# Gate rows moved from GpSimd to VectorE, dwo tiles and loads in another order: one change to a fused attention and MLP gradient kernel

## The chip, the cores and the metric

The kernel runs on one core of a Trainium2 chip. A core has five engines, each with its own instruction queue: TensorE (PE, matmuls; PEld are its weight loads), VectorE (DVE), ScalarE (ACT), GpSimd (POOL) and SyncE (SP, which here only issues DMAs). Matmul results land in PSUM, a small accumulation memory; everything else is in SBUF or in device memory. An engine runs its own queue in order and waits for others by semaphores. The metric is the time of one execution in device microseconds; a run gives the median of several executions.

## What is computed

The reference is the forward pass and all gradients of a block that multiplies an attention branch with a gated MLP branch (2048 rows, 512 channels, 32 heads of 16, hidden size 1792):

```python
def _A_ref(x, wqkv, wo):                       # attention
    q, k, v = split_heads(x @ wqkv)
    p = softmax(einsum("bhqd,bhkd->bhqk", q, k) * Dh ** -0.5)
    return merge_heads(einsum("bhqk,bhkd->bhqd", p, v)) @ wo
def _B_ref(x, w1, b1, w2, b2):                 # MLP
    h = gelu(layernorm(x) @ w1 + b1)
    return h @ w2 + b2
xn  = layernorm(x)
out = x + _A_ref(xn, wqkv, wo) * silu(_B_ref(xn, w1, b1, w2, b2))
# results: out, and the gradients of x, wqkv, wo, w1, b1, w2, b2 for a given grad_out
```

## The kernel before

Rows are handled in 16 tiles of 128 ("row t"), in four groups of four. The program has three parts, each written in a fixed order by hand; nothing is rescheduled.

**First part (`Pre`).** It projects q, k and v and transposes them, computes the MLP's hidden layer (`hid`) and then runs a loop over the 16 rows. For row t, `gate(t)` does 14 matmuls into `ps_m`, adds the bias on DVE (L373), takes tanh on ACT (L374) and runs a chain of three DVE instructions (L375 to L377): `sg`, the gate `G_`, and `dsr`, which is grad_out times the gate (dSO). `gate_b` then makes the gradient factor `B_` with four instructions on POOL (L381 to L384). Two rows later `dproj` multiplies the transposed dSO (`dsoT`) with wo to get dO: four matmuls into `ps_do`, a DVE cast into `ndc` (L393) and a POOL copy into `ND` (L394). `t_do` and `t_ds` transpose dO and dSO on PE, with a copy on ACT (L177). `gate_store` writes `gbr` (GB_s) and `dsr` (DSO_s) to device memory for every second row; `after` writes a group's dO (NATQd_s, DOT_s) and then loads the first head pair's share back (`op0["do"]`, L95 and L98). All these DMAs go through SP's queue, except the last `gate_store`, which goes through POOL's. The gate_b of rows 14 and 15 is kept in a list and issued at the end. An ACT instruction on one element (L446) loads the table for the exponential ahead of attention; it stands behind row 15's tanh.

The tiles `gbr`, `dOT` and `gd` (whose halves are `gw`, with `m_` and `sg`, and `dsr`) have memory that attention's `ek` tiles take over: the first write of such a tile waits for the last reader and the last store of the old one.

**Attention (`attention_core`).** 1024 steps: scores (L1083), exponential on ACT (L1092), dP (L1105) and its product on DVE (L1122), PE transposes (L1167) with their copies into `ek` (L1179), and accumulating matmuls. SP issues DMA transposes of `gts` and `ets`. POOL clears the second operand set first (L47 to L50) and then loads the next head pair, paced by the steps.

**Tail (`Grads.run`).** Rows 2 to 15: `emit_so(t)` multiplies the attention output with wo (`ps_so`), DVE makes `dm_all` (L573) and `t13` (L575), POOL adds x and stores the output for two rows (L584, L586; a ring of two tiles). `emit_oT` and `emit_dmT` are PE transposes with ACT copies. `load_s1` loads the rows' factors. Between rows, four tiles of the gradient of wo (`emit_dwo`, 16 matmuls each, needs all of `dso_all`) are emitted after rows 9, 11, 13 and 14. Then follow 14 tiles of dw2 (`emit_dw2`, each needs an `hgr` tile that SP loads with a DMA transpose, L698), dwq and dwkv (12 tiles, the latter need `dKVn`, eight DMA transposes, L781), and the groups dh (need `w2T`, 14 DMA transposes, L778), dy (need `w1T`, L853), dw1 and dx. Alongside, `slope_step` issues one piece of the derivative of gelu: 49 pieces over 16 chunks of h1 (`load_h1`), with Square and Sigmoid on ACT (L654, L668, L669) and multiplications on DVE (L658 to L675).

All loads of the tail are on SP's queue in the order of the program text, so a load that waits (for its memory to come free, or for an earlier DMA) holds up all behind it.

Of the kernel before, what the change touches and what calls it, by code (L numbers as in the profile page):

```python
# [11 lines left out]
ALU = mybir.AluOpType  # L12
# [89 lines left out]
class Pre:  # L102


    def __init__(self, ctx, tc, k, op0, A_x, A_wqkv, A_wo, B_w1, B_b1, B_w2, B_b2, grad_out):
# [257 lines left out]
        def gate(t):  # L363
            g, t4 = t // 4, t % 4
            ps = psA.tile([128, 512], f32, name="ps_m", tag="mm")
            for fc in range(FC):
                nc.tensor.matmul(ps[:], lhsT=hgT[:, g % 2, fc, t4 * 128:(t4 + 1) * 128], rhs=w2_sb[:, fc, :],  # L367
                                 start=(fc == 0), stop=(fc == FC - 1))
# [5 lines left out]
            nc.scalar.activation(out=ta, in_=m_, func=ACT.Tanh, scale=0.5)  # L374
            nc.vector.tensor_scalar(out=sg, in0=ta, scalar1=0.5, scalar2=0.5, op0=ALU.mult, op1=ALU.add)  # L375
            nc.vector.tensor_tensor(out=G_, in0=m_, in1=sg, op=ALU.mult)
            nc.vector.tensor_tensor(out=dsr[:, t % 4, :], in0=dot, in1=G_, op=ALU.mult)  # L377
            return lambda: gate_b(B_, G_, sg, dot)

        def gate_b(B_, G_, sg, dot):  # L380
            nc.gpsimd.tensor_scalar(out=B_, in0=sg, scalar1=-1.0, scalar2=1.0, op0=ALU.mult, op1=ALU.add)  # L381
            nc.gpsimd.tensor_tensor(out=B_, in0=B_, in1=G_, op=ALU.mult)
            nc.gpsimd.tensor_tensor(out=B_, in0=B_, in1=sg, op=ALU.add)
            nc.gpsimd.tensor_tensor(out=B_, in0=B_, in1=dot, op=ALU.mult)  # L384

        def t_ds(t):
            tp(lambda b: dsr[:, t % 4, b * 128:(b + 1) * 128], dsoT[:, t % 2], 0)
# [8 lines left out]
        def t_do(t):  # L396
            g = (t // 4) % 2
            tp(lambda b: ndc[:, t % 2, b * 128:(b + 1) * 128], dOT[:, g, :, (t % 4) * 128:(t % 4) * 128 + 128], 0)

        def after(t):  # L400
            if t % 4 == 3:
                g = t // 4
                ld(out=k.NATQd_s[:, :, g * 4:g * 4 + 4, :].rearrange("a p t c -> p a t c"), in_=ND[:, g % 2])
                ld(out=k.DOT_s.rearrange("(c p) s -> p c s", p=128)[:, :, g * 512:(g + 1) * 512], in_=dOT[:, g % 2])
                op0["do"](g)

        def gate_store(t, ld=ld):
            if t % 2 == 1:
                ld(out=k.GB_s.rearrange("(t p) x d -> p t x d", p=128)[:, t - 1:t + 1], in_=gbr[:, (t - 1) % 4:(t - 1) % 4 + 2])
                ld(out=k.DSO_s.rearrange("(t p) d -> p t d", p=128)[:, t - 1:t + 1], in_=dsr[:, (t - 1) % 4:(t - 1) % 4 + 2, :])  # L410

        def load_dot(g):
            ld(out=dotr[:, g % 2], in_=go2[:, g * 4:g * 4 + 4])
# [11 lines left out]
        for t in range(NT):  # L425
            g, t4 = t // 4, t % 4
            n0, n1 = (0, 4, 8, 11, 14)[t4:t4 + 2]
            if g < 3:
                for fc in range(n0, n1):
                    hid(g + 1, fc)  # L430
            if t == 4:
                op0["q"]()
            if t >= 1:
                gate_store(t - 1)
            if t == 0:
                bound()
            gb = gate(t)
            if t == 0:
                stores_nat(3)
            if t < 14:  # L440
                gb()
            else:
                lastb.append(gb)
            if t == 15:

                nc.scalar.activation(out=b2bc[0:1, 0:1], in_=b2bc[0:1, 0:1], func=ACT.Exp)  # L446
            if t >= 2:
                dproj(t - 2)
            if t >= 3:
                t_do(t - 3)  # L450
                after(t - 3)
            if t >= 1:
                t_ds(t - 1)
            if t4 == 3 and g + 2 < 4:
                load_dot(g + 2)
            if 2 <= t < 6:
                wkv_rows(t - 2)
        dproj(NT - 2)
        t_do(NT - 3)
        after(NT - 3)  # L460
        t_ds(NT - 1)
        t_do(NT - 2)
        after(NT - 2)
        dproj(NT - 1)
        t_do(NT - 1)
        after(NT - 1)
        for gb in lastb:
            gb()
        gate_store(NT - 1, nc.gpsimd.dma_start)


GA = 0.044715
# [4 lines left out]
class Grads:  # L477
# [119 lines left out]
    def run(self):  # L597
# [99 lines left out]
        def load_hg(fc):  # L697
            tr(out=hgr[:, fc % 4], in_=k.HGT_s[fc * 128:fc * 128 + 128, :])  # L698
# [37 lines left out]
        self.load_s1(2)  # L736
        self.load_s1(3)
        self.load_s1(4)
        load_h1(0, 0)
        load_h1(0, 1)  # L740
        nc.vector.memset(ones_bf[:], 1.0)

        nd = 0
        for t in range(2, NT):
            self.emit_so(t)
            if t + 2 < NT:
                self.emit_oT(t + 2)
            while nd < t and nd <= 2 * (t - 3) + 1:
                emit_dmT(nd)
                nd += 1  # L750
            if t == 3:
                self.load_s1(5)
                ld(out=dso_all[:, 0:8], in_=dsov[:, 0:8])
            if t == 5:
                self.load_s1(6)
                ld(out=dso_all[:, 8:16], in_=dsov[:, 8:16])
                load_h1(0, 2)
            if t == 7:
                self.load_s1(7)
                load_hg(0)  # L760
            if t in (9, 11, 13, 14):
                i = (9, 11, 13, 14).index(t)
                emit_dwo(i)
                (load_hg(i + 1) if i < 3 else load_h1(1, 1))
                (load_h1(0, 3) if i == 0 else load_h1(1, 0) if i == 2 else None)
        self.flush_adds()
        while nd < NT:
            emit_dmT(nd)
# [62 lines left out]
        for i in range(12):  # L831
# [635 lines left out]
```

## Time and profile before

| | us |
|---|---|
| median of three runs | 2234.59 (2231.56 to 2238.38) |
| profiled execution, whole | 2229.55 |
| its span, first to last instruction | 2227.8 |
| mean granted TensorE clock | 0.993 of full speed |

The profile records one execution. A row of a timeline has the start in us from the span's start, the length in us, the engine, the line, the operation, what it writes and reads with its shapes, and the count if neighbours are merged; in brackets stands the idle time of the engine ahead of it and what ended it. "SPq" rows are DMA issues on SP's queue. A row of the windows gives a stretch, its length, the busy time of PE, PEld, DVE, ACT and POOL with instruction counts, the granted PE clock, the DMA engines' busy share and GB/s. The chain of waits follows the work that ended last back from the end.

### The profile page before, as it was taken

The page shows a single profiled execution, that of the slowest core. Times are in us where ns is not written, and L with a number is a line of the kernel's source. Part 1 is how long each engine was busy: PE and PEld are TensorE (multiplying, and loading weights), DVE is VectorE, ACT ScalarE, POOL GpSimd, SP SyncE. Part 2 cuts the span into 40 slices and gives each one's busy share as a digit, 9 for nine tenths or more (in the row PEclk, how much of TensorE's full clock was granted, in tenths as well). Part 3 has the DMA queues.
Part 4 walks back from the last instruction along what each step waited for, and adds up shares of the span by engine and source line. Part 5 has one row for each costly group of instructions (what it writes and reads, how often), then busy time and mean ns, then how long its engine had stood idle before and what let it go on. Part 6 is the DMA issues. An engine that isn't in the chain of part 4 may idle for free.

```text
span 2227.8 us, 74213 instructions
## 1 busy us (share of the span) xinstructions
PE 2158.9 (97%) x30690; PEld 1204.8 (54%) x30690; DVE 1912.6 (86%) x3626; ACT 1734.3 (78%) x2481; POOL 607.5 (27%) x1387
## 2 busy tenths in 40 slices
PE   6999899999999999999999999999999999899998
PEld 3444455555555555555555555555555555344444
DVE  6676799999999999999999999999999998698624
ACT  5664888888888888888888888888888886584214
POOL 4276413222222222222312222222213223310002
PEclk9999999999999999999999999999999999999999
DMA  7785999999999999999999999999999999899874
GB/s 230 245 275 197 190 200 192 199 203 194 202 201 196 201 192 210 196 204 196 202 201 198 200 194 204 197 195 204 199 201 200 196 213 230 233 251 252 231 202 155
DMA packets 1421747, 461.15 MB, mean 207 GB/s; under 512 B 1334622, under 2 KB 1405662, under 8 KB 1421408
## 3 DMA queue, kind: packets, MB, share of 16 engines
q1 hardware_dynamic: 1406880, 424.67, 100.3%
q0 software_dynamic: 12944, 30.16, 5.2%
q8 instruction: 240, 3.93, 0.8%
q10 hardware_dynamic: 1584, 1.57, 0.2%
q14 instruction: 99, 0.81, 0.1%
HBM read 62.79 MB, written 64.75 MB: 57 GB/s over the span
## 4 chain that ended last, share of the span: by engine, by line
PE 89%; DVE 3%; DMA 3%; ACT 3%; issue 2%; SPq 1%; POOL 1%; DVEq 0%; ACTq 0%; POOLq 0%
PE tT L1167 24%; PE d L1105 14%; PE X L1197 10%; PE Z L1281 10%; PE X L1200 5%; PE X L1204 5%; PE s L1083 2%; PE ps_dw L729 2%; PE ps_dy L902 2%; PE ps_m L367 2%; PE ps_h L352 2%; PE ps_dw L974 2%; PE ps_dh L868 2%; PE XT L1223 1%; PE ps_qkv L210 1%
## 5 line engine op out<-in xcount | busy, mean ns | idle before, releaser
L1122 DVE TENSOR_TENSOR gts<-d,ets 128x512 bf16<-128x512 f32 x2048 | 1363.0, 684 | 99.5 <-ACT ek L1179 20.3
L1092 ACT ACTIVATE ets<-s 128x1024 bf16<-128x1024 f32 x1024 | 1048.7, 1024 | 196.9 <-PE s L1083 94.6
L1167 PE MATMUL tT<-ident_bf,ets 128*128 128x128 bf16 x7168 | 569.2, 219 | 15.9 <-ACT ek L1179 6.1
L1167 PEld LDWEIGHTS <-ets 128*128 128x128 bf16 x7168 | 445.7, 97 | 241.2 <-issue 239.3
L1179 ACT COPY ek<-tT 128x448 f32<-128x448 f32 (+2 forms) x1024 | 501.6, 490 | 7.3 <-DVE ek L1179 6.1
L1105 PE MATMUL d<-QDT,KVT 32*128 32x512 bf16 x2048 | 457.4, 385 | 0.0
L1083 PE MATMUL s<-QDT,KVT 32*128 32x512 bf16 x2048 | 401.3, 380 | 3.0 <-ACT ets L1092 2.7
L1105 PEld LDWEIGHTS <-KVT 32*128 32x128 bf16 x2048 | 145.2, 91 | 323.7 <-issue 323.7
L1197 PE MATMUL X<-ets,NAT 128*32 128x256 bf16 x4096 | 300.5, 284 | 0.1
L1204 PE MATMUL X<-gts,NAT 128*17 128x256 bf16 x4096 | 289.8, 273 | 0.0
L1200 PE MATMUL X<-ets,Lc 128*32 128x256 bf16 x4096 | 289.8, 273 | 0.0
L1341 POOL COPY tick<-gts 1x2 bf16<-1x2 bf16 x205 | 36.1, 176 | 604.5 <-DVE gts L1122 604.5
L1281 PE MATMUL Z<-gk,W 128*32 128x512 bf16 x2048 | 197.8, 379 | 1.0 <-DVE acc L1295 1.0
L1281 PE MATMUL Z<-ek,W 128*32 128x512 bf16 x1792 | 198.6, 379 | 0.0
L1246 POOL TENSOR_TENSOR W<-NATQq,rL 128x128 bf16<-128x128 bf16 x64 | 25.4, 397 | 525.2 <-DVE rL L1245 442.5
L1197 PEld LDWEIGHTS <-NAT 128*32 128x32 bf16 x4096 | 106.1, 93 | 110.9 <-issue 11.6
L1083 PEld LDWEIGHTS <-KVT 32*128 32x128 bf16 x2048 | 138.8, 91 | 11.2 <-issue 8.6
L1179 DVE COPY ek<-tT 128x64 f32<-128x64 f32 (+1 forms) x576 | 132.4, 230 | 4.8 <-DMA DSO_s<-gd 3.5
L1281 PEld LDWEIGHTS <-W 128*32 128x32 bf16 x4096 | 109.7, 97 | 11.5 <-issue 1.5
L1200 PEld LDWEIGHTS <-Lc 128*32 128x32 bf16 x4096 | 107.9, 96 | 0.0
L1204 PEld LDWEIGHTS <-NAT 128*17 128x17 bf16 x4096 | 103.5, 92 | 3.1
L1281 PE MATMUL Z<-ekd,W 128*32 128x512 bf16 x256 | 97.0, 379 | 0.0
(244 smaller groups left out, 2340.9 us busy)
## 6 DMA issues: line engine op xcount, KB each, us to landing
gk<-gts SPq DMA_TRANSPOSE x512, 5.2
H1T_s<-h1r SPq DMA_DIRECT2D x28, 256.0 KB, 4.0
HGT_s<-hgT SPq DMA_DIRECT2D x8, 896.0 KB, 4.5
DH_s<-stg SPq DMA_DIRECT2D x12, 512.0 KB, 3.4
hch<-DH_s SPq DMA_DIRECT2D x12, 512.0 KB, 4.4
gp<-H1T_s SPq DMA_DIRECT2D x9, 512.0 KB, 5.5
out_dram<-ob_w POOLq DMA_DIRECT2D x36, 128.0 KB, 4.3
NAT_s<-NS SPq DMA_DIRECT2D x4, 1056.0 KB, 6.1
```

Source lines behind the costliest of these rows:

```text
L352: nc.tensor.matmul(ps[:], lhsT=w1_sb[:, ic, fc * 128:(fc + 1) * 128], rhs=yT[:, ic, g * 512:(g + 1) * 512], start=(ic == 0), stop=(ic == I ...
L367: nc.tensor.matmul(ps[:], lhsT=hgT[:, g % 2, fc, t4 * 128:(t4 + 1) * 128], rhs=w2_sb[:, fc, :], start=(fc == 0), stop=(fc == FC - 1))
L1083: nc.tensor.matmul(s[:, hj, :], lhsT=op["KVT"][r:r + 32, kb * 128:(kb + 1) * 128], rhs=op["QDT"][r:r + 32, qc * 512:(qc + 1) * 512], start ...
L1092: nc.scalar.activation(out=st_et[g][:, :, :, a[1] % 4, :].rearrange("k b h q -> k h b q"), in_=cur["s"][:].rearrange("k h (b q) -> k h b q ...
L1105: nc.tensor.matmul(d[:], lhsT=op["KVT"][r:r + 32, kb * 128:(kb + 1) * 128], rhs=op["QDT"][r:r + 32, qc * 512:(qc + 1) * 512], start=True, ...
L1122: nc.vector.tensor_tensor(out=gts[:, kb % 2, hj, :].rearrange("k (b q) -> k b q", b=4), in0=st_d.pop((g, hj))[:].rearrange("k (b q) -> k b ...
L1167: nc.tensor.transpose(t[:, i, :], et[:, b // 2, b % 2, kk, :], ident_bf[:])
L1179: copy(out=blk[j]["Ek"][kb // 4][:, kb % 4, lo:hi].rearrange("q i k -> q (i k)").bitcast(f32), in_=st_T[g][:, lo:hi].rearrange("q i k -> q ...
L1197: nc.tensor.matmul(X[r:r + 32, 0:256], lhsT=NATt[:, kb, hj, 1:33], rhs=ev, start=(kb == 0), stop=False, skip_group_check=True, tile_positi ...
L1200: nc.tensor.matmul(X[r:r + 32, 256:512], lhsT=Lc[:], rhs=ev, start=False, stop=False, skip_group_check=True, tile_position=(0, r))
L1204: nc.tensor.matmul(X[r:r + 17, 256:512], lhsT=NATt[:, kb, hj, 0:17], rhs=gv, start=False, stop=(kb == 15), skip_group_check=True, tile_pos ...
L1281: nc.tensor.matmul(Z[r:r + 32, :], lhsT=WT[j % 2][1 - part][:, qb, hj, :], rhs=mv, start=(part == 0 and qb == 0), stop=(part == 1 and qb = ...
```

## The change

In the first part, gate_b of rows 13, 14 and 15 is issued on VectorE instead of GpSimd: row 13's and row 14's in the loop one row later (behind that row's `dproj`), row 15's at the end. Row 15's chain of three is issued behind the cast of `dproj(13)`. The store of rows 12 and 13 moves behind gate_b 13. After the loop the transposes of dO 13 and dSO 15 come first, then the store of dSO rows 14 and 15 (now on SP's queue), the table load for the exponential, and both last `dproj` back to back. The store of the gate rows 14 and 15 stands on SP's queue between the last group's dO stores and their loads.

In the tail, `dso_all`'s first half is loaded ahead of all h1 chunks, its second half where it was; the four dwo tiles follow rows 12 to 15; the first four `hgr` loads follow rows 8 to 11; the h1 chunks are loaded in order at other places. During dw2 no `w2T` is loaded: all fourteen are loaded during dwkv. The early dw2 tiles take one slope piece instead of two at two places, so that 45 of the 49 pieces, not 47, are issued ahead of dh.

```diff
@@ gate
             nc.scalar.activation(out=ta, in_=m_, func=ACT.Tanh, scale=0.5)
-            nc.vector.tensor_scalar(out=sg, in0=ta, scalar1=0.5, scalar2=0.5, op0=ALU.mult, op1=ALU.add)
-            nc.vector.tensor_tensor(out=G_, in0=m_, in1=sg, op=ALU.mult)
-            nc.vector.tensor_tensor(out=dsr[:, t % 4, :], in0=dot, in1=G_, op=ALU.mult)
-            return lambda: gate_b(B_, G_, sg, dot)
+            def chain():
+                nc.vector.tensor_scalar(out=sg, in0=ta, scalar1=0.5, scalar2=0.5, op0=ALU.mult, op1=ALU.add)
+                nc.vector.tensor_tensor(out=G_, in0=m_, in1=sg, op=ALU.mult)
+                nc.vector.tensor_tensor(out=dsr[:, t % 4, :], in0=dot, in1=G_, op=ALU.mult)
+            if t < NT - 1:
+                chain()
+            return chain, lambda e: gate_b(e, B_, G_, sg, dot)
@@ gate_b: the four instructions on the engine e instead of nc.gpsimd
@@ after
-        def after(t):
+        def after(t, f=lambda: None):
...
                 ld(out=k.DOT_s.rearrange("(c p) s -> p c s", p=128)[:, :, g * 512:(g + 1) * 512], in_=dOT[:, g % 2])
+                f()
                 op0["do"](g)
@@ gate_store is split into gb_store (GB_s) and dso_store (DSO_s)
@@ the loop over rows
-            if t >= 1:
+            if 1 <= t < 14:
                 gate_store(t - 1)
...
-            gb = gate(t)
+            chain, gb = gate(t)
-            if t < 14:
-                gb()
+            if t < 13:
+                gb(nc.gpsimd)
             else:
                 lastb.append(gb)
-            if t == 15:
-                nc.scalar.activation(out=b2bc[0:1, 0:1], in_=b2bc[0:1, 0:1], func=ACT.Exp)
             if t >= 2:
                 dproj(t - 2)
+            if t == 14:
+                lastb[0](nc.vector)
+                gate_store(13)
+            if t == NT - 1:
+                chain()
+                lastb[1](nc.vector)
@@ behind the loop
+        t_do(NT - 3)
+        t_ds(NT - 1)
+        dso_store(NT - 1)
+        nc.scalar.activation(out=b2bc[0:1, 0:1], in_=b2bc[0:1, 0:1], func=ACT.Exp)
         dproj(NT - 2)
-        t_do(NT - 3)
-        after(NT - 3)
-        t_ds(NT - 1)
+        dproj(NT - 1)
         t_do(NT - 2)
-        after(NT - 2)
-        dproj(NT - 1)
         t_do(NT - 1)
-        after(NT - 1)
-        for gb in lastb:
-            gb()
-        gate_store(NT - 1, nc.gpsimd.dma_start)
+        lastb[2](nc.vector)
+        after(NT - 1, lambda: gb_store(NT - 1))
@@ Grads.run, rows 2 to 15
         self.load_s1(4)
-        load_h1(0, 0)
-        load_h1(0, 1)
+        ld(out=dso_all[:, 0:8], in_=dsov[:, 0:8])
...
             if t == 3:
                 self.load_s1(5)
-                ld(out=dso_all[:, 0:8], in_=dsov[:, 0:8])
+                load_h1(0, 0)
             if t == 5:
                 self.load_s1(6)
                 ld(out=dso_all[:, 8:16], in_=dsov[:, 8:16])
-                load_h1(0, 2)
+                load_h1(0, 1)
             if t == 7:
                 self.load_s1(7)
-                load_hg(0)
-            if t in (9, 11, 13, 14):
-                i = (9, 11, 13, 14).index(t)
-                emit_dwo(i)
-                (load_hg(i + 1) if i < 3 else load_h1(1, 1))
-                (load_h1(0, 3) if i == 0 else load_h1(1, 0) if i == 2 else None)
+                load_h1(0, 2)
+            if t in (8, 9, 10, 11):
+                load_hg(t - 8)
+            if t >= 12:
+                emit_dwo(t - 12)
+                load_h1((t - 9) // 4, (t - 9) % 4)
@@ Grads.run, dw2
             if fc % 2 == 0 and fc >= 2:
-                load_h1(1 + (fc + 2) // 8, ((fc + 2) // 2) % 4)
+                n = 7 + (fc - 2) // 2
+                load_h1(n // 4, n % 4)
...
-            if fc >= 10:
-                load_w2T(nw)
-                nw += 1
...
-            slope_step(1 + (fc % 2 or fc < 4))
+            slope_step(1 + fc % 2)
@@ Grads.run, dwq and dwkv
-            if i in (0, 2, 4, 6):
-                load_h1(3, i // 2)
+            if i < 3:
+                load_h1(3, 1 + i)
...
-            if 4 <= i <= 8:
+            if 4 <= i <= 10:
                 for _ in range(2):
                     if nw < FC:
                         load_w2T(nw)
```

More of the change, by code (lines that the diff above doesn't have):

```diff
@@ L374, in gate, with gate_b @@
             nc.scalar.activation(out=ta, in_=m_, func=ACT.Tanh, scale=0.5)
-            nc.vector.tensor_scalar(out=sg, in0=ta, scalar1=0.5, scalar2=0.5, op0=ALU.mult, op1=ALU.add)
-            nc.vector.tensor_tensor(out=G_, in0=m_, in1=sg, op=ALU.mult)
-            nc.vector.tensor_tensor(out=dsr[:, t % 4, :], in0=dot, in1=G_, op=ALU.mult)
-            return lambda: gate_b(B_, G_, sg, dot)
[L380 to L384, printed above, removed]
+            def chain():
[5 more added lines that the diff above has]
+            return chain, lambda e: gate_b(e, B_, G_, sg, dot)
+        def gate_b(e, B_, G_, sg, dot):
+            e.tensor_scalar(out=B_, in0=sg, scalar1=-1.0, scalar2=1.0, op0=ALU.mult, op1=ALU.add)
+            e.tensor_tensor(out=B_, in0=B_, in1=G_, op=ALU.mult)
+            e.tensor_tensor(out=B_, in0=B_, in1=sg, op=ALU.add)
+            e.tensor_tensor(out=B_, in0=B_, in1=dot, op=ALU.mult)
         def t_ds(t):
@@ L404, in after, with gate_store, gb_store, dso_store @@
                 ld(out=k.DOT_s.rearrange("(c p) s -> p c s", p=128)[:, :, g * 512:(g + 1) * 512], in_=dOT[:, g % 2])
+                f()
                 op0["do"](g)
-        def gate_store(t, ld=ld):
+        def gate_store(t):
             if t % 2 == 1:
-                ld(out=k.GB_s.rearrange("(t p) x d -> p t x d", p=128)[:, t - 1:t + 1], in_=gbr[:, (t - 1) % 4:(t - 1) % 4 + 2])
-                ld(out=k.DSO_s.rearrange("(t p) d -> p t d", p=128)[:, t - 1:t + 1], in_=dsr[:, (t - 1) % 4:(t - 1) % 4 + 2, :])
+                gb_store(t)
+                dso_store(t)
+        def gb_store(t):
+            ld(out=k.GB_s.rearrange("(t p) x d -> p t x d", p=128)[:, t - 1:t + 1], in_=gbr[:, (t - 1) % 4:(t - 1) % 4 + 2])
+        def dso_store(t):
+            ld(out=k.DSO_s.rearrange("(t p) d -> p t d", p=128)[:, t - 1:t + 1], in_=dsr[:, (t - 1) % 4:(t - 1) % 4 + 2, :])
         def load_dot(g):
```

## The prediction

> **What bounds the kernel now.** I read the page first (busy shares, chain of waits), then the timeline of each engine in the two places that the diff touches, then windows for the granted clock. TensorE (PE) sets the time nearly everywhere:
>
> ```profile
> span 2227.8 us, 74213 instructions
> PE 2158.9 (97%) x30690; PEld 1204.8 (54%) x30690; DVE 1912.6 (86%) x3626; ACT 1734.3 (78%) x2481; POOL 607.5 (27%) x1387
> PE 89%; DVE 3%; DMA 3%; ACT 3%; issue 2%; SPq 1%; POOL 1%; DVEq 0%; ACTq 0%; POOLq 0%
> ```
>
> So only idle PE time, or PE time at a reduced clock, can be won. Three places have it. **Place 1**, the seam from the first part to attention (timelines of PE, ACT, DVE, POOL, SP; then windows):
>
> ```profile
> 207.88 3.19 PE L367 MATMUL ps_m<-w_sb,hgT 128*128 128x512 bf16 x14
> 216.46 1.04 PE L392 MATMUL ps_do<-woT,dsoT 128*128 128x512 bf16 x4 [3.16 <-ACT dsoT L177]
> 238.27 0.91 PE L1167 MATMUL tT<-ident_bf,ets 128*128 128x128 bf16 x7 [3.36 <-ACT ek L1179]
> ...
> 213.96 1.28 ACT L446 ACT_TABLE_LOAD   x1
> 222.71 1.03 ACT L1092 ACTIVATE ets<-s 128x1024 bf16<-128x1024 f32 x1
> 252.99 1.02 ACT L1092 ACTIVATE ets<-s 128x1024 bf16<-128x1024 f32 x1 [0.17 <-PE s L1083]
> ...
> 208.77 1.21 DVE L375 TENSOR_SCALAR gd<-tau 128x512 bf16<-128x512 f32 x1 [0.83 <-ACT tau L374]
> 214.05 0.43 DVE L375 TENSOR_SCALAR gd<-tau 128x512 bf16<-128x512 f32 x1 [0.83 <-ACT tau L374]
> 237.44 0.23 DVE L1179 COPY ek<-tT 128x64 f32<-128x64 f32 x1 [3.52 <-DMA DSO_s<-gd]
> ...
> 208.55 1.15 POOL L383 TENSOR_TENSOR gbr<-gbr,gd 128x512 bf16<-128x512 bf16 x1
> 232.09 0.73 POOL L410 DMA_DIRECT2D DSO_s<-gd  x1
> 232.82 1.82 POOL L47 MEMSET KVT<- 128x2048 bf16 x1
> ...
> 222.92 0.89 SPq L404 DMA_DIRECT2D DOT_s<-dOT  x1
> 227.11 0.79 SPq L95 DMA_DIRECT2D QDT<-DOT_s  x2
> ...
> core 0: us, PE busy (x) PEld busy (x) DVE busy (x) ACT busy (x) POOL busy (x), PEclk, DMA share, GB/s
> 222.00:232.00 10.00, 7.62 (x87) 3.64 (x85) 5.29 (x9) 6.94 (x10) 9.22 (x10) 0.66 0.71 154
> 238.00:242.00 4.00, 3.73 (x46) 2.02 (x45) 2.99 (x7) 3.01 (x5) 2.70 (x5) 0.59 0.78 178
> ```
>
> The last gate row's matmuls end near 211, but the first exponential of attention runs only at 222.71: the table load sits ahead of the copy (dsoT) that PE waits 3.16 us for. Then PE stops 3.36 us at 238.27: attention's ek tile lies in the memory of gd, and gd's last store leaves POOL's queue only at 232.09, behind the eight gate_b instructions of rows 14 and 15. Each stop is followed by a stretch at reduced clock (0.66, 0.59). **Places 2 and 3**, the tail:
>
> ```profile
> 1899.48 2.95 PE L719 MATMUL ps_dwo<-dso_all,Oall 128*128 128x512 bf16 x8 [2.40 <-DMA dso_all<-DSO_s]
> 1905.47 3.57 PE L719 MATMUL ps_dwo<-dso_all,Oall 128*128 128x512 bf16 x8 [3.04 <-DMA dso_all<-DSO_s]
> 1921.98 0.38 PE L562 MATMUL o_tp<-ident_bf,Oall 128*128 128x128 bf16 x4 [2.73 <-ACT oT L564]
> 1935.07 0.40 PE L706 MATMUL dm_tp<-ident_bf,dm_all 128*128 128x128 bf16 x4 [2.00 <-DVE dm_all L573]
> 1935.71 48.52 PE L729 MATMUL ps_dw<-dm_all,hgr 128*128 128x512 bf16 x224
> 1999.67 13.97 PE L820 MATMUL ps_dwkv<-dKVn,xn 128*128 128x512 bf16 x64 [1.63 <-ACT ob_w L714]
> 2015.50 13.97 PE L820 MATMUL ps_dwkv<-dKVn,xn 128*128 128x512 bf16 x64 [1.86 <-DMA dKVn<-dKVT_s]
> ...
> 1897.00:1909.00 12.00, 6.57 (x18) 2.37 (x18) 3.81 (x5) 4.32 (x4) 3.56 (x4) 0.63 1.10 357
> ```
>
> Place 2 is dwo: four idle times before dw2 begins, 2.40 + 3.04 + 2.73 + 2.00 = 10.2 us, and the clock at 0.63. Place 3 is the two waits for dKVn.
>
> **Part by part: the seam.** The change takes gate_b of rows 13 to 15 from POOL to DVE: 12 instructions, at the 0.43 of the 214.05 row about 0.45 us each with issue, so 1.75 us a row. POOL's contention goes with them: at 208.77 the same instruction took 1.21 beside POOL's 208.55. I walk the new order. Row 14's chain then takes 1.4 us from 208.7, the cast of dO 12 ends near 210.7, gate_b 13 near 212.4; only then comes row 15's add, at 212.4 instead of 212.6: no loss. Tanh ends at 213.6, the cast of dO 13 stands ahead of chain 15, which ends near 215.1; PE transposes it until 215.5 and runs both last dproj back to back to 217.3. The table load now lies beside them. DVE casts both after gate_b 14 (to 216.8), so until 218.1; the transposes and ACT copies end at 219.0. First exponential at 219.1: **3.6 us gained** (bounds 1.5, when one more 1.2 us contention hits each of two links, and 4.5). Gate_b 15 ends near 220, when the first multiply is due.
>
> SP's queue: the stores of rows 12 and 13 now wait for gate_b 13 on DVE, some 1.4 us later than before, and behind them NATQd, dO and the loads of dO; the 222.92 and 227.11 rows give 4.2 us from a dO store to the load behind it. In the new order the second-last group's loads go at 218.5, the last dSO store at 220, the last dO store at 221, landing near 225.3; the gate store stands behind it. The ek copy is due 3.6 us earlier than its 233.9 (237.44 less 3.52), near 230.3. Margin 5 us: the stop goes, **3.3 us** (bounds 2.0 and 3.4), and with it the second slow stretch: 4 us at 0.59, of which I take **1.0**. The first slow stretch stays; PE is half idle from 217 to 221. Since the seam is ahead of a PE-bound loop (0.17 before the exponential of 252.99, sixteen steps on), nothing behind it takes the gain back.
>
> One contention is new: POOL, free earlier, clears KVT and QDT (1.82 us each) from 218.8, beside gate_b 15. Bounds from the kernel's start:
>
> ```profile
> 5.16 3.65 POOL L50 MEMSET KVT<- 1x2048 bf16 x2
> 6.54 0.16 DVE L189 TENSOR_TENSOR lnv<-mv,rstd 128x2 f32<-128x2 f32 x1
> 7.41 1.55 DVE L195 TENSOR_SCALAR xt<-xt,mv,rstd 128x512 bf16<-128x512 bf16 x1
> ```
>
> A one-input instruction was held until the memset's end (8.8), a two-input one ran through in 0.16. So gate_b's first may lose up to 1.8 us, its other three nothing; it starts at 218.1, ahead of the memset, and I take 0. The Trainium skill (SBUF — State Buffer, "Who interferes with whom") says that a GpSimd instruction shuts out VectorE's two-port modes for its whole length, and two-input ones only if it reads SBUF, which a memset doesn't. By the same sentence POOL's copies to ND, which do read SBUF, would hold up gate_b 13 and 14 as well; no row here shows such a pair, and priced by 208.77 against 214.05 it is 0.8 us each, for a result of 2213.5.
>
> **Dwo.** The tiles move behind rows 12 to 15 and dso_all's first half ahead of all h1 loads; the second half, landed at 1905.4 before, has 0.5 MB less ahead. PE's work here starts with row 2:
>
> ```profile
> 1882.09 1.04 PE L571 MATMUL ps_so<-wo_sb,oT 128*128 128x512 bf16 x4
> ```
>
> From there to 1935.7 there are 53.6 us: less 10.2 and 0.4 of small waits, and less 3.7 of slow clock (2.95 and 3.57 for eight matmuls against 1.73 at full clock, and 0.8 in the next row), 39.3 are work. What is late next:
>
> ```profile
> 1893.87 0.73 POOL L586 DMA_DIRECT2D out_dram<-ot  x1 [0.30 <-POOL ot L584]
> 1900.82 1.70 POOL L584 TENSOR_TENSOR ot<-t,s1x 128x512 bf16<-128x512 f32 x1 [1.67 <-DVE sl L658]
> ```
>
> POOL's add of row 8 waits for the buffer stored at 1893.87; it ends at 1902.0, and DVE's rows 10 and 11 queue behind it. PE reaches row 11's transposes at 1901.6, but dm_all 11 comes at 1903.4: a new wait of 1.8 us (0 if the store lands early, 5 if the next store is as slow). The first dwo tile then starts at 1904, needs the second half at 1905.7, and dw2 begins at 1882.1 + 39.3 + 1.8 = 1923.2. ACT has 21 us of slope, evacuation and copies in these 21, but two transpose buffers and five PSUM tiles cover its lag. **Gain 12.4** (9 to 14.3).
>
> The Trainium skill (TensorE: Matmul & The Clock Gate, Part 1) has the clock halve only after an idle window of about 3.4 us. By that the gaps here, at most 3.04, would cost no clock and the gain would be 3.7 smaller, for 2215.5; the 0.63 of the quoted window contradicts it, so the measurement decides.
>
> **dKVn and w2T.** Four w2T transposes leave the queue ahead of dKVn; all fourteen stand behind it:
>
> ```profile
> L781 SPq DMA_TRANSPOSE dKVn<-dKVT_s x8: 2037/3225/4127, 1981.7 to 2009.2; - x8
> ...
> 1972.46 3.56 SPq L698 DMA_TRANSPOSE hgr<-HGT_s  x1
> 2012.56 5.19 SPq L778 DMA_TRANSPOSE w2T<-in_B_w_dram  x4
> 2029.56 10.36 SPq L853 DMA_TRANSPOSE w1T<-in_B_w_dram  x4
> ...
> 2041.81 13.11 PE L868 MATMUL ps_dh<-dmT,w2T 128*128 128x512 bf16 x60 [0.68 <-DVE db1acc L871]
> 1946.23 0.69 DVE L659 TENSOR_TENSOR sl<-sl,gp 128x1024 bf16<-128x1024 bf16 x1
> ```
>
> Call E the end of dw2 (1984.2 before). The L781 row gives minimum, median and maximum ns of a transpose on SP. SP starts its last hgr at E − 11.8 and took 40.1 us until the last dKVn was issued; four w2T at 5.19/4 less leave 34.9. The first four dKVn land near E + 10, due at E + 13.9; the last near E + 25, due at E + 27.8. Both waits go: **3.5** (0 to 3.5). The w2T run from E + 23 to E + 50 with y_all and two w1T (10.36/4) between; the last is due at E + 53 and lands near it. Two slope steps of half size move into the first dh group, four DVE instructions of at most 0.69 us, where PE already waited 0.68. For both I take **−1.0** (−3 to 0).
>
> **Sum.** 3.6 + 3.3 + 1.0 + 12.4 + 3.5 − 1.0 = 22.8 us. The profiled execution took 2229.6 (2227.8 and 1.8 around it): 2206.8. It lies 5.0 under the runs' median of 2234.6, so the forecast for the median is 2212.
>
> **Rivals.**
> (a) The seam gives nothing: if all four instructions of gate_b 15 were held by a memset each (4 × 1.82), DVE reaches its first multiply at 226 instead of 220 and 6 of the 7.9 are lost: 2218. The 7.41 row speaks for, the 6.54 row against. 0.10.
> (b) Dwo keeps its waits: row 8's add waited 7 us for a store; if rows 10 to 15 each wait so, POOL sets the pace and 7 of 12.4 are lost: 2219. For it: DMA share 1.10; against: the queue is lighter. 0.10.
> (c) Nothing measurable: the same bytes pass at a DMA share near 1, so what PE wins it waits out at dKVn and hgr; 18 lost, 2230. Against: SP sat idle 10 us before dw2. 0.05.
> (d) Slower: w2T is late for dh. At 1.3 us each it just fits. At m each PE waits 14 × (m − 1.3) − 1; this eats all from m = 3.0. dKVn's transposes took 3.2, and at 4.1 each (their longest) it is 38 us: 2250. Against: the quoted four took 5.19 together. 0.05.
>
> **How the numbers follow.** Forecast 0.70. Its own bounds: gains 10 to 26, so 2208 to 2225, and 3 for the runs' spread below. With (a) and (b) inside, the range is 2205 to 2225. A measurement tells 0.3% (6.7 us) from no change: faster 0.70 + 0.10 + 0.10 = 0.90, same 0.05, slower 0.05.
>
> **What would show it.** First exponential near 219; no DVE wait on the dSO store; no dso_all wait, granted clock 1.0 around the dwo tiles, dw2 starting 12 us earlier relative to the end of attention; no dKVn wait; at most 3 us of PE idle in the first dh group. A stop at ek, a POOL-paced row or a wait for w2T would make it wrong.

## The result, and the profile after

| | median us | runs | before, same chip | ratio, 95% interval |
|---|---|---|---|---|
| changed kernel | 2213.60 (2212.67 to 2214.71) | 4 | 2236.48 | 0.9901 (0.9883 to 0.9920) |

The changed kernel is 22.9 us faster by the medians (forecast 2212). The profiled executions lie closer together: 2229.55 before, 2212.67 after, 16.9 us. That difference matters below. The top of the page of the changed kernel:

```profile
span 2210.8 us, 74213 instructions
PE 2154.0 (97%) x30690; PEld 1203.2 (54%) x30690; DVE 1911.7 (86%) x3638; ACT 1734.2 (78%) x2481; POOL 590.4 (27%) x1373
```

PE's busy time fell by 4.9 us (2158.9 before) though it has as many matmuls: that part of the gain is clock. The seam, from the timelines of PE, ACT, DVE and POOL of the changed kernel (line numbers are about 10 higher than before):

```profile
208.60 3.19 PE L367 MATMUL ps_m<-w_sb,hgT 128*128 128x512 bf16 x14
216.43 0.61 PE L173 MATMUL tp_ps<-ident_bf,gd 128*128 128x128 bf16 x4 [1.48 <-DVE gd L379]
216.83 3.06 PE L396 MATMUL ps_do<-woT,dsoT 128*128 128x512 bf16 x8
...
221.66 1.03 ACT L1102 ACTIVATE ets<-s 128x1024 bf16<-128x1024 f32 x1
247.80 1.02 ACT L1102 ACTIVATE ets<-s 128x1024 bf16<-128x1024 f32 x1
...
211.67 0.71 DVE L386 TENSOR_TENSOR gbr<-gbr 128x512 bf16<-128x512 bf16 x1
212.42 0.42 DVE L387 TENSOR_TENSOR gbr<-gbr,gd 128x512 bf16<-128x512 bf16 x1
214.66 0.80 DVE L377 TENSOR_SCALAR gd<-tau 128x512 bf16<-128x512 f32 x1 [0.16 <-ACT tau L374]
222.13 0.42 DVE L388 TENSOR_TENSOR gbr<-gbr,dotr 128x512 bf16<-128x512 bf16 x1
233.07 0.22 DVE L1189 COPY ek<-tT 128x64 f32<-128x64 f32 x1
...
211.50 0.61 POOL L398 COPY ND<-nat 128x512 bf16<-128x512 bf16 x1 [2.76 <-DVE nat L397]
214.56 0.61 POOL L398 COPY ND<-nat 128x512 bf16<-128x512 bf16 x1 [2.45 <-DVE nat L397]
221.31 1.80 POOL L47 MEMSET KVT<- 128x2048 bf16 x1
```

The ek copy no longer waits for a store (233.07 has no bracket). The first exponential comes at 221.66, only 1.05 us earlier than before. Row 15's matmuls ran 0.7 us later in this execution, and so did already row 0's (113.4 against 112.7), where the code is the same; the seam itself gained 1.8. The eight matmuls of the last two dproj took 3.06 us. The windows of the changed kernel (length, busy time of five engines, granted clock, DMA share, GB/s) show why:

```profile
213.10:216.80 3.70, 0.76 (x8) 0.59 (x9) 3.44 (x8) 2.08 (x4) 0.61 (x1) 0.86 0.72 238
216.80:219.90 3.10, 3.10 (x15) 1.30 (x12) 1.78 (x4) 2.07 (x3) 0.29 (x1) 0.61 1.09 308
223.30:230.10 6.80, 5.70 (x70) 2.86 (x67) 4.07 (x7) 4.53 (x6) 5.29 (x4) 0.55 0.85 253
230.10:240.00 9.90, 9.84 (x156) 5.36 (x145) 9.57 (x20) 9.19 (x15) 0.73 (x3) 1.00 1.21 207
```

PE is nearly idle for 3.7 us and then has 0.61 of its clock just when both dproj run. The first slow stretch of attention is still there (0.55), the second is gone (1.00 from 230 to 240, where it was 0.59). The tail, PE's timeline of the changed kernel:

```profile
1877.82 1.04 PE L584 MATMUL ps_so<-wo_sb,oT 128*128 128x512 bf16 x4
1899.56 0.40 PE L719 MATMUL dm_tp<-ident_bf,dm_all 128*128 128x128 bf16 x4 [1.52 <-DVE dm_all L586]
1900.20 3.63 PE L732 MATMUL ps_dwo<-dso_all,Oall 128*128 128x512 bf16 x16
1919.37 48.73 PE L742 MATMUL ps_dw<-dm_all,hgr 128*128 128x512 bf16 x224
1998.09 13.97 PE L830 MATMUL ps_dwkv<-dKVn,xn 128*128 128x512 bf16 x64 [2.37 <-DMA dKVn<-dKVT_s]
2023.45 6.22 PE L878 MATMUL ps_dh<-dmT,w2T 128*128 128x512 bf16 x28 [1.03 <-DMA w2T<-in_B_w_dram]
2030.18 7.93 PE L878 MATMUL ps_dh<-dmT,w2T 128*128 128x512 bf16 x36 [0.51 <-DVE db1acc L881]
```

From row 2 to dw2 are 41.55 us, 12.1 less than the 53.6 before. The dwo tiles run without a wait at full clock (3.63 us for sixteen matmuls), and the new wait at dm_all 11 is there with 1.52 us. The second wait for dKVn has stayed.

### The profile page after: what moved, and what is told of

It reads as the page before. It is cut to its first block, busy times and chain, and to the rows that moved or that the text cites. A ratio compares the mean times of both kernels' runs of the same rounds, so it can differ in the third digit from the quotient of the medians.

```text
span 2210.8 us, 74213 instructions
## 1 busy us (share of the span) xinstructions
PE 2154.0 (97%) x30690; PEld 1203.2 (54%) x30690; DVE 1911.7 (86%) x3638; ACT 1734.2 (78%) x2481; POOL 590.4 (27%) x1373
## 4 chain that ended last, share of the span: by engine, by line
PE 89%; DVE 4%; ACT 2%; issue 2%; DMA 2%; POOL 1%; SPq 1%; ACTq 0%; DVEq 0%; POOLq 0%
PE tT L1177 24%; PE d L1115 15%; PE X L1207 10%; PE Z L1291 10%; PE X L1210 5%; PE X L1214 5%; PE s L1093 3%; PE ps_dw L742 2%; PE ps_dy L912 2%; PE ps_h L352 2%; PE ps_dw L984 2%; PE ps_m L367 2%; PE ps_dh L878 2%; PE XT L1233 1%; PE ps_qkv L210 1%
## 5 line engine op out<-in xcount | busy, mean ns | idle before, releaser
L1351 POOL COPY tick<-gts 1x2 bf16<-1x2 bf16 x205 | 35.7, 174 | 612.3 <-DVE gts L1132 612.3
```

## Experiments

All kernels compute all of the reference; b1 and c2 do 15 matmuls more. Each was timed beside runs of the kernel before on the same chip. Its median there was 2234.24 us beside e1 to e4 (the row "before"), 2237.10 beside the kernels named b and 2237.73 beside those named c; a close comparison is best made within one of these groups. To see where time goes, the table divides one profiled execution of each into four stretches, read off the timelines and the views of single tiles: A from the start of row 15's last `ps_m` matmul to the 17th exponential of attention; B from there to the first `ps_so` matmul; C to the first dw2 matmul; D to the first dy matmul. For the kernel before A runs from 210.7 to 252.99 and C + D ends at 2054.8; for the changed one 211.4, 247.80 and 2038.0.

| kernel | median us (range, runs) | A | B | C | D |
|---|---|---|---|---|---|
| before | 2234.24 (2229.48 to 2244.97, 16) | 42.3 | 1621.5 | 61.2 | 119.1 |
| changed | 2213.60 (2212.67 to 2214.71, 4) | 36.4 | 1622.5 | 49.1 | 118.6 |
| changed, again (c1) | 2214.16 (2211.38 to 2215.28, 4) | 35.7 | 1623.9 | 48.4 | 119.4 |
| new seam, old tail (e1) | 2225.56 (2221.35 to 2232.96, 10) | 35.9 | 1624.6 | 60.0 | 121.7 |
| old seam, new tail (e2) | 2221.06 (2219.86 to 2222.62, 6) | 43.6 | 1624.8 | 48.2 | 118.2 |
| new loads, dwo early (e3) | 2222.67 (2220.38 to 2231.09, 7) | 35.4 | 1621.5 | 60.9 | 119.1 |
| old loads, dwo late (c4) | 2212.25 (2211.49 to 2218.38, 4) | 36.0 | 1625.0 | 48.4 | 122.6 |
| four w2T early (e4) | 2214.40 (2212.28 to 2214.88, 6) | 36.4 | 1624.1 | 49.0 | 119.7 |
| gate_b on POOL (b2) | 2214.59 (2213.18 to 2218.65, 4) | 39.5 | 1624.9 | 48.3 | 121.7 |
| unread matmuls (b1) | 2220.19 (2215.33 to 2220.89, 5) | 34.6 | 1626.7 | 48.7 | 120.5 |
| the same again (c2) | 2224.94 (2216.58 to 2232.09, 6) | 34.7 | 1632.6 | 48.8 | 123.7 |
| dKVn first (b4) | 2213.65 (2209.05 to 2222.62, 6) | 37.1 | 1622.4 | 48.6 | 116.8 |
| t13 a row later (b5) | 2213.57 (2211.36 to 2215.20, 4) | 36.0 | 1623.3 | 47.1 | 120.9 |
| b4 and b5 (c3) | 2209.67 (2205.95 to 2211.69, 4) | 35.3 | 1624.8 | 47.8 | 117.5 |

The stretch B, whose code is the same in all, ranges from 1621.5 to 1625.0 without the two kernels of the unread matmuls, so a difference of up to 3.5 us there between two profiles says nothing. The profiled execution was the longest of its kernel's runs for b2, c3 and c4 (2218.65, 2211.69, 2218.38) and the shortest for the changed kernel, b1, b4, b5 and c1, so stretches and medians don't answer to each other closely.

**The two halves.** e1 is the kernel before with the change's first-part hunks, e2 with its tail hunks.

> The change's first part alone; the tail is that of before. My account from the two traces: row 2 of the tail starts 4.3 us earlier (1877.82 against 1882.09), so this kernel should take 4 to 5 us off, a ratio near 0.998. Rival 1 (the seam as I forecast it): 7.9 us, ratio 0.9965. Rival 2 (the parts interact: the seam pays only with the new tail): 0 to 1 us. Beside it: the runs of before spread over 7 us and those of the changed kernel over 2. If what varies is the seam of before (the stop at ek behind the store on POOL's queue), this kernel spreads over 2 to 3 us and gains more against the median than against the fast end, 8 to 10 us.

> The change's tail alone; the first part is that of before. If the parts add and the traces tell it rightly, 12.1 us from row 2 to the first dw2 tile and 0.5 to 1 behind it: 12.6 to 13 us off, ratio near 0.9942. Rival (what varies between runs of before lies in the tail, its waits for dso_all): 16 to 18 us off the median, ratio 0.992, and runs that lie within 2 us of each other.

The seam is worth more than I read off the one pair of traces. e1's ratio is 0.9958 (0.9940 to 0.9976), 5 to 13 us. It is measured more closely by e2 against the changed kernel, which spread little: 2221.06 less 2213.60 and 2214.16, 6.9 to 7.5 us (against e4, on e2's chip, 6.7). Stretch A agrees: 42.3 and 43.6 with the old seam, 36.0 on the mean of the nine with the new one (b1, b2 and c2 left out), 6.9 less. The tail's ratio is 0.9939 (0.9923 to 0.9955), 13.2 us by the medians, where the theory had 12.6 to 13. e1 spreads over 11.6 us, like the kernel before, and e2 over 2.8: on this chip what varies between executions goes with the old tail, not with the stop at ek.

**Place or loads.** e3 puts the tiles back and keeps the loads; c4 has the old order of loads and only moves the tiles:

```diff
@@ e3, against the changed kernel
-            if t >= 12:
-                emit_dwo(t - 12)
+            if t in (9, 11, 13, 14):
+                emit_dwo((9, 11, 13, 14).index(t))
@@ c4, against e1
             if t in (9, 11, 13, 14):
                 i = (9, 11, 13, 14).index(t)
-                emit_dwo(i)
...
+            if t >= 12:
+                emit_dwo(t - 12)
```

> The changed kernel with its new order of loads, but with the four dwo tiles back behind rows 9, 11, 13 and 14. In the changed trace the second half of dso_all lands at 1897.5 (issued at 1891.2, 6.3 to landing) and the tile behind row 9 would need it near 1895.5: a wait of 2 us that the changed kernel doesn't have, and behind it the waits for oT (2.7) and dm_all (2.0) of before come back, while the 1.5 of dm_all 11 goes. Theory (the late tiles pay by themselves): 3 to 6 us slower than the changed kernel, 2217 to 2220. Rival (the earlier load of dso_all is what paid, the place of the tiles is worth nothing): within 1 us of the changed kernel, 2213 to 2215.

> The other half of the experiment with early dwo tiles: the old order of loads throughout the tail, with the new first part, and only the four dwo tiles moved behind rows 12 to 15. With the new loads and the old places the stretch from the first ps_so to the first dw2 tile was 60.9 us, as in the kernel before (61.2), against 49.1 with both. Theory (the place is all of it): 48.5 to 51 us, dso_all's second half landing near 31 us behind the first ps_so, when the first tile is due; 2213.5 to 2217. Rival (each needs the other: with the old loads the first tile waits for dso_all): over 53 us in the stretch, 2218 or more.

The place is all of it: C is 60.9 with the new loads and early tiles, 48.4 with the old loads and late ones. And c4's median is no higher than that of the changed kernel on the same chip (2212.25 against c1's 2214.16): the new order of loads as a whole is worth nothing that these runs show. PE's timeline of e3:

```profile
1895.45 3.23 PE L732 MATMUL ps_dwo<-dso_all,Oall 128*128 128x512 bf16 x8 [4.66 <-DMA dso_all<-DSO_s]
1912.16 0.58 PE L575 MATMUL o_tp<-ident_bf,Oall 128*128 128x128 bf16 x4 [3.99 <-ACT oT L577]
1926.43 0.40 PE L719 MATMUL dm_tp<-ident_bf,dm_all 128*128 128x128 bf16 x4 [2.01 <-DVE dm_all L586]
```

Waiting 4.7 us for dso_all and then 4.0 for ACT's oT, it lost 8.3 to 9.1 us against e4, c1 and the changed kernel, more than I expected. (The 6.3 us to landing in the expectation are those of dso_all's first half; in e3 the second half was issued at 1886.72, and PE could go on with it only at 1895.45, 8.7 us later.) PE's timeline of c4 has no such wait; from 1900 to 1921 PE is busy for 20.93 of the 21 us:

```profile
1897.16 0.40 PE L719 MATMUL dm_tp<-ident_bf,dm_all 128*128 128x128 bf16 x4 [1.20 <-DVE dm_all L586]
1901.48 3.63 PE L732 MATMUL ps_dwo<-dso_all,Oall 128*128 128x512 bf16 x16
1920.65 11.61 PE L742 MATMUL ps_dw<-dm_all,hgr 128*128 128x512 bf16 x53
```

A dwo tile gives PE 3.6 us of work that needs nothing from the rows around it; behind rows 12 to 15 it stands where dso_all has landed and where oT and dm_all would be waited for. (c4's profile is its slowest run, 2218.38, with two waits for dKVn in D.)

**The queue of loads.** e4 puts four w2T loads back into dw2:

```diff
+            if fc >= 10:
+                load_w2T(nw)
+                nw += 1
             if fc >= 11:
                 load_dkv(0, fc - 11)
...
-            if 4 <= i <= 10:
+            if 4 <= i <= 8:
```

> The changed kernel with four of the fourteen w2T loads back in dw2 (behind its tiles 10 to 13). They take about 5.2 us of SP's queue ahead of dKVn. Theory (SP's queue is what makes dKVn late): the second wait for dKVn grows from 2.4 to 5 to 7 us in all or is split between both halves, and the 1.0 us wait for w2T in dh goes: 2 to 4 us slower than the changed kernel, 2216 to 2218. Rival (dKVn's second half waits for its memory to come free, not for the queue): no difference, 2213 to 2214.

By its number the rival held: 2214.40, a wait for dKVn of 2.8 us instead of 2.4, and none for w2T. Taking w2T out of dw2 was worth nothing measurable. The rival's reason (memory that comes free late) isn't shown by this, and the next kernel speaks against it. b4 changes what stands around dKVn's second half; b5 takes DVE's queue out of the wait at dm_all; c3 does both:

```diff
@@ b4
-            if i < 3:
-                load_h1(3, 1 + i)
-            if 1 <= i <= 4:
-                load_dkv(1, i - 1)
+            if i < 2:
+                load_dkv(1, 2 * i)
+                load_dkv(1, 2 * i + 1)
+            if 2 <= i < 5:
+                load_h1(3, i - 1)
...
-            if i >= 8:
-                j = i - 8
+            if i == 11:
+                for j in range(IC):
                     tr(out=w1T[:, :, j, :], in_=self.B_w1[j * 128:j * 128 + 128, :])
@@ b5: in emit_so, from row 2 on
-        t1 = self.row("t13")
-        nc.vector.tensor_tensor(out=t1[:], in0=ps[:], in1=g[:, t % 2, 0, :], op=ALU.mult)
+        if self.held:
+            self.emit_t13(*self.held.pop())
+        self.held.append((t, ps, g, x))
```

> The changed kernel with the four loads of dKVn's second half ahead of the last three h1 loads, and the four w1T loads behind all w2T. The changed kernel waits 2.4 us for dKVn's second half and 1.0 for w2T. Theory (order on SP's queue decides): the first dKVn of the second half is issued as soon as dw2 has freed its memory; both waits go, 2 to 3.4 us off, 2210 to 2212. Rival (SP and the DMA engines are full here, about 3.1 us for each of these transposes; or the first of them waits for dwq as its row shows, 2.5 us): the wait shrinks by the 1.8 us of the three h1 loads at most, or not at all, and the time by 0 to 1.5 us.

> The changed kernel, in which DVE makes t13 of row t behind dm_all of row t+1 (from row 8 on), so that a t13 which waits for POOL's add doesn't hold the next dm_all. The forecast named the new wait at dm_all 11 (1.8 us) and the trace has 1.52 there. Theory (DVE's queue hands POOL's wait on to PE): the 1.52 us wait goes or falls under 0.3, 1 to 1.5 us off, 2212 to 2212.6. Rival (the dwo tiles behind need the second half of dso_all or ACT's oT, and the wait only moves there): no difference in the time, dw2 starts 49 us behind the first ps_so as now.

> The changed kernel with dKVn's second half ahead of the h1 loads, w1T behind w2T, and t13 a row later. In the profiles the first took the stretch from the first ps_so to the first dy from 167.7 to 165.3 us, the second left it at 168.0 and only moved the wait from dm_all to hgr. Theory (SP's queue and the DMA engines pace the stretch; only an order that puts the urgent transposes first wins): 165 to 166 us in the stretch, 2 us off the changed kernel's median, 2211 to 2212. If both add: 163.5 and 2210. Rival (the waits move on whatever is done): no difference beyond 1 us.

SP's timeline of the changed kernel, and then of b4:

```profile
1978.24 0.53 SPq L657 DMA_DIRECT2D gp3b<-H1T_s  x1
1978.86 0.45 SPq L657 DMA_DIRECT2D gp3c<-H1T_s  x1
1979.42 5.17 SPq L793 DMA_TRANSPOSE dKVn<-dKVT_s  x1
1984.65 0.57 SPq L657 DMA_DIRECT2D gp3d<-H1T_s  x1
1985.27 9.18 SPq L793 DMA_TRANSPOSE dKVn<-dKVT_s  x3
```

```profile
1967.03 19.61 SPq L793 DMA_TRANSPOSE dKVn<-dKVT_s  x7
```

In b4 the last dKVn has left SP at 1986.64, in the changed kernel at 1994.45: 6.6 us earlier, counted from the end of dw2 (1966.8 and 1967.9). PE's waits for dKVn and w2T are gone; D falls to 116.8, in the shortest of its six runs. Its median doesn't show the gain: 2213.65, and 2213.12 without the one run of 2222.62, where the theory had 2210 to 2212. By the time the rival held, by the waits the theory. In b5 the dm_all wait is gone (C 47.1), but its median is no lower (2213.57), and the waits of PE in its tail are now these:

```profile
PE ps_dw L753 <- DMA hgr<-HGT_s: 2.3, 2, 1.3
PE ps_dwkv L842 <- DMA dKVn<-dKVT_s: 1.7, 1, 1.7
```

What C won, D gave back, much of it to the hgr loads: the wait only moved, as the rival had it, though further on than it named. Together they seem to pay: c3 took 2209.67 against 2214.16 for the changed kernel on the same chip, 4.5 us less, with a ratio of 0.9878 (0.9863 to 0.9893) to the kernel before. With four runs each and 0.3 us of overlap that is likely, not certain. The profile doesn't show the two adding: C and D are 165.3 us together, as in b4, where 163.5 was expected if both add and the changed kernel has 167.7. So 2.4 us of the 4.5 are found there, and the rest isn't placed. It is the lowest median here.

**The seam.** b2 keeps the new order but has the three gate_b on POOL (`lastb[i](nc.gpsimd)`). b1 and c2 (the same kernel twice) give PE, at the places where it waits, matmuls whose result nobody reads:

```diff
+        warm(6)
         t_do(NT - 3)
+        warm(6)
         t_ds(NT - 1)
...
         t_do(NT - 2)
+        warm(3)
         t_do(NT - 1)
```

> The changed kernel in its new order, but with gate_b of rows 13, 14 and 15 on POOL at the same places of the program. Theory (POOL's work beside DVE's is what the move of gate_b takes away): one-input instructions of the chain of rows 14 and 15 take up to 1.2 us beside POOL, and the copies to ND and the last gate store queue behind 12 POOL instructions of 1.15 us; the first exponential 1 to 2.5 us later, the stop at ek comes back in part: 2 to 5 us slower than the changed kernel, 2216 to 2219. Rival (the new order of stores, table load and dproj is all that pays): within 1 us of the changed kernel, or faster by up to 1 because DVE is free of 5.2 us of work.

> The changed kernel with 15 matmuls whose result nobody reads, placed where PE waits in the seam: six ahead of the transposes of dO 13, six ahead of those of dSO 15, three between the last two transposes of dO. In the changed kernel the eight matmuls of the last two dproj take 2.8 to 3.06 us at a granted clock of 0.70, against 1.73 at full clock, and the first exponential runs 10.1 us behind the start of the last ps_m matmul, 1.9 earlier than in the kernel before, where I had forecast 3.6. Theory (the idle PE loses its clock, and the slow dproj takes back what the shorter DVE chain won): the eight matmuls take 1.8, the first exponential is 1.2 to 1.5 earlier (8.6 to 8.9 behind), 1.2 to 3 us off the changed kernel, 2210.5 to 2212.5. Rival (DVE sets the time of the casts, PE's clock is covered): the first exponential within 0.3 of 10.1 and the time within 0.5 us.

> The kernel with the 15 unread matmuls in the seam once more. Its seam was 1.6 us shorter at the 16th step of attention (34.6 us behind the last ps_m against 36.2 on the mean of the six others with this seam), but its median was 6 us above the changed kernel's and its attention 4 us longer in the one profile. Theory (the shorter seam makes DMA transposes of attention late at more of its steps: a fixed property of this order): again 2217 to 2221, and the profile's attention over 1625 us from the 16th exponential on. Rival (an accident of those runs): 2211 to 2213, attention 1622 to 1624.

> The changed kernel as it is, so that the others of this call stand beside it on one chip: 2212.5 to 2215, all its runs within 3 us of each other, and about 22 us under the kernel before.

b2's DVE timeline shows what the move to DVE takes away:

```profile
213.27 0.43 DVE L377 TENSOR_SCALAR gd<-tau 128x512 bf16<-128x512 f32 x1 [1.76 <-POOL gbr L387]
213.73 1.25 DVE L378 TENSOR_TENSOR gbr<-gd 128x512 bf16<-128x512 bf16 x1
```

DVE stands 1.76 us behind POOL's instruction, and the next takes 1.25 where it takes 0.42 alone. The first exponential comes 12.1 us behind the last `ps_m` matmul, as in the kernel before (12.0), against 10.3 in the changed one. Of these 1.8 us, 1.3 are a later start of the last dproj (6.7 us behind the last `ps_m` matmul, against 5.4); the rest is the clock, since the eight matmuls took 3.62 instead of 3.06, which b4 had too, with gate_b on DVE. The stop at ek stays away, so it went with the new order of the stores and not with gate_b's engine. A is 3.5 longer than the mean of 36.0, but in b2's longest run; its median is 0.9 to 1.0 us above b4's and b5's on the same chip, and so by the time the rival held: what moving gate_b to DVE pays by itself, these runs don't tell from nothing.

c1 is the changed kernel once more, and its seam went otherwise. PE's and ACT's timelines of it, then its windows:

```profile
214.50 1.93 PE L396 MATMUL ps_do<-woT,dsoT 128*128 128x512 bf16 x8
218.20 1.03 ACT L1102 ACTIVATE ets<-s 128x1024 bf16<-128x1024 f32 x1
```

```profile
211.00:214.50 3.50, 0.64 (x9) 0.47 (x10) 3.24 (x8) 2.08 (x4) 0.62 (x1) 1.00 0.71 241
214.50:216.50 2.00, 1.98 (x12) 0.66 (x10) 1.82 (x4) 1.73 (x2) 0.05 (x1) 1.00 1.25 311
219.50:226.40 6.90, 5.79 (x60) 2.88 (x55) 4.30 (x7) 4.53 (x6) 5.64 (x5) 0.53 0.91 275
```

The same program, as idle ahead of dproj (0.64 us busy in 3.5), kept its clock there: 1.93 us instead of 3.06, and the first exponential at 9.0 us behind the last `ps_m` matmul (209.2) instead of 10.3. Only the slow stretch in attention came (0.53). The Trainium skill (TensorE: Matmul & The Clock Gate, Part 1) says that the hardware judges PE's activity in windows of 3.4 us that run freely and don't start with the kernel. These two executions agree that the program alone doesn't fix the clock; no run here shows the length of a window.

The same eight matmuls tell the kernels with this seam apart. They start 5.3 to 5.4 us behind the last `ps_m` matmul in all nine (b1, b2 and c2 left out), and where they take 1.93 us (c1, c3, c4) the first exponential comes at 9.0 us, where they take 2.78 to 3.06 (changed, b5, e1, e3, e4) at 10.0 to 10.3, and in b4, at half clock, at 11.0. PE's timeline of b4:

```profile
214.84 3.62 PE L396 MATMUL ps_do<-woT,dsoT 128*128 128x512 bf16 x8
```

With the unread matmuls dproj ran at full clock in both profiles (1.93 us, first exponential at 9.0, A 34.6 and 34.7), and the kernel was 6.6 and 10.8 us slower than the changed one all the same, where b1's theory had it 1.2 to 3 faster. B grew to 1626.7 and 1632.6, and in c2 D to 123.7. One place in B, the timelines of ACT and SP of c2:

```profile
625.99 1.02 ACT L1110 ACTIVATE ets<-s 128x1024 bf16<-128x1024 f32 x1 [2.30 <-DMA ekd<-ets]
617.72 1.34 SPq L1172 DMA_TRANSPOSE ekd<-ets  x1
619.15 11.00 SPq L1156 DMA_TRANSPOSE gk<-gts  x3
```

The exponential waits for the transfer that still reads the ets tile it is to overwrite; the last one issued ahead of it, at 617.72, landed some 8 us later, beside three transposes that held SP for 11.0 us. Over attention from about its 17th exponential on, the waits of ACT in c2 and then in the changed kernel (us in total, times, longest):

```profile
ACT ets L1110 <- DMA ekd<-ets: 13.3, 12, 2.3
```

```profile
ACT ets L1102 <- DMA ekd<-ets: 4.8, 7, 1.0
```

PE in turn waits 7.7 us for these exponentials in c2, against 1.2 in the changed kernel, so most of c2's longer B is idle PE behind late transposes. The exponential shown is that of the 252nd step. This step is late in both profiles with the unread matmuls (1.7 and 2.1 us beside the shortest time of the same step in the other profiles), so it isn't an accident of one run. But b2, whose seam ends 3.5 us later, is late there too (2.1), with 10.4 us of such waits of ACT in all and a B of only 1624.9. And c1, c3 and c4, whose first exponential comes as early as with the unread matmuls (9.0), didn't get slower. So the theory that a shorter seam makes the transposes late isn't borne out; what brings it on is open.

## Why the prediction was right, and where luck helped

The forecast of 2212 is 1.6 us off, but that it is so close is luck: two errors nearly cancel. The sum against the profiled execution gave 2206.8, and 2212.67 was measured, 5.9 more. I then added 5.0 because before's profiled run lay that far under its median; after's lies only 0.9 under its own. So the medians differ by 22.9, near the sum of 22.8, while the two executions that the sum was about differ by 16.9. Where the offset comes from is not shown. Side by side on one chip, the kernels with early dwo tiles spread over 10.7 to 15.5 us (before, e1, e3) and e2 and e4, with late ones, over 2.8 and 2.6; that fits waits for DMA in the early tiles. But before and e1 have more runs, before spreads over 6.4 to 9.2 beside the other kernels, and with the changed tail as it is b2 spreads over 5.5 and c2 over 15.5.

By the steps of the prediction:

- **Seam, first exponential (3.6 forecast).** 1.8 in this profile and 3.0 in its repeat. The order on DVE went as walked. The step that failed is "PE runs both last dproj back to back to 217.3": it assumed full clock, though the forecast itself had PE half idle there. Over the nine profiles with this seam the gain is 1.0 to 3.1 us and follows the length of these eight matmuls (3.62 to 1.93 us); what decides their clock in an execution is not shown. Of the 1.8 missing here, 1.2 were lost to the clock. The other 0.6 has one measured part: chain 15 was held by POOL's copy to ND (0.80 at 214.66, where 0.43 is usual).
- **Seam, ek and the second slow stretch (3.3 and 1.0).** Right: the stop and the stretch are gone. From the first to the 17th exponential 30.3 us before (222.71 to 252.99), 26.1 after: 4.1 in this pair. Whole seam: 7.9 forecast, 5.9 in this pair, 6.9 over all profiles. The stop stayed away in b2 too, so the new place of the stores ends it; the contention with POOL that the forecast credits to gate_b's move is there in b2's profile, but its time doesn't show it.
- **POOL beside DVE.** Gate_b 15's two-input instruction at 222.13 took 0.42 beside the memset of 221.31, so rival (a) fell (its one-input instruction, at 220.61, ran ahead of the memset). POOL's copies do hold two-input instructions: 0.71 at 211.67 beside the copy of 211.50, against 0.42. That bears out the Trainium skill (SBUF — State Buffer, "Who interferes with whom"), by which a two-input VectorE instruction contends with a GpSimd instruction that reads SBUF. The price is 0.3 to 0.4 us a place, not the 0.8 that I took from the 208.77 row, where POOL's instruction was twice as long. The trace of before had such a pair, which I overlooked: DVE's L377 at 211.31 took 0.72 beside POOL's copy of 210.94 (L394).
- **Dwo (12.4).** (The working's own figures, 53.6 less 41.1, give 12.5.) 12.1 in this pair, and the new wait as forecast (1.8; 1.52). What I credited to the earlier load of dso_all is worth nothing: with the old loads (c4) the stretch is as short. Rival (b) fell with the 12.1.
- **dKVn and w2T (3.5 less 1.0).** Mis-sized: 0.5 in this pair (D 119.1 to 118.6). Over all profiles the gain isn't clear of the spread: D is 118.2 to 123.7 in the six with the changed tail as it is (mean 120.4; b1, b2 and c2 among them) and 119.1 to 122.6 in the three with the old loads (before, e1, c4; mean 121.1), and by time c4 is as fast as c1. I charged SP's queue with the w2T that left it, and not with the h1 loads that stayed between dKVn's, nor with a wait ahead of the second half: 5.17 us for one transpose, of which the waits of SP put 2.5 down to dwq. e4 shows that the w2T in dw2 cost nothing measurable; in b4's and c3's profiles another order around dKVn takes the waits away. Dh's waits, 1.03 and 0.51, were inside the bound.
- **Not in the sum:** row 15 ran 0.7 us later and attention took 1.0 longer. With 2.0 for the seam, 0.3 for dwo, 2.0 for the loads and 0.2 the other way at the end, that is 5.8 of the 5.9.

Rivals (c) and (d) fell: no measured kernel with the new tail waited over 2.8 us for w2T.

## What to carry to other kernels

A profiled time and a median differ by what varies between executions (5.0 us before, 0.9 after), so the offset of one kernel isn't to be carried over to the forecast of another. Where a block of PE work can stand late in a loop without being needed, its place can be worth more than any order of its loads: 12 us here, against nothing measurable. Taking one wait out of a stretch whose loads fill one queue may only move it, as in b5; putting the transfer that PE needs next ahead of the others took both waits away in b4 and c3, and in c3 the time probably with them.

## What was not expected of the hardware

The granted clock in the seam differed between two executions of one program (0.61 and 1.00 for the same eight matmuls, 3.06 and 1.93 us). PE at 84% busy (5.70 of 6.80 us, at 223.30) didn't win its clock back for almost 7 us. And the kernel whose unread matmuls keep PE busy in the seam, with both dproj at full clock in its two profiles, was 6 to 11 us slower; in c2 ACT's waits for DMA transposes, from some 400 us further on, were 8.5 us longer in total. Why those transposes were late is open.
